# Second score half and second exponential moved ahead of the first sums and the first logarithm in a 64-step recurrent attention

## The chip, the core and the metric

The kernel runs on one core of one Trainium2 chip. The core has five engines with an instruction queue each: PE (TensorE, matmuls), ACT (ScalarE), DVE (VectorE), POOL (GpSimd) and SP (SyncE, which only issues transfers here). They are tied together by semaphores alone. The metric is the time of one execution on the device in microseconds (us), as the median of several runs; lower is better.

## The reference

The reference has two parts. A is an attention with a recurrent memory: the sequence of 2048 rows is cut into 64 segments of 32 rows, and each segment attends to itself and to 8 memory rows. The first 8 rows of a segment's output are the memory of the next, so the 64 steps can only run one after the other. B, a gated MLP with spatial mixing, comes after A and is not touched by the change.

```python
# A, cut: S 2048, Dm 512, H 32 heads, Dh 128, M 8 memory rows, seg_len 32
for s in range(n_seg):
    xs = x[:, s * seg_len:(s + 1) * seg_len, :].copy()
    h = jnp.concatenate([mem, xs], axis=1)
    q = jnp.einsum('btd,dhe->bhte', h, Wq)
    k = jnp.einsum('btd,dhe->bhte', h, Wk)
    v = jnp.einsum('btd,dhe->bhte', h, Wv)
    scores = jnp.einsum('bhqe,bhke->bhqk', q, k) * scale
    scores = jnp.where(mask[None, None], scores, -1000000000.0)
    p = _softmax(scores, axis=-1)
    o = jnp.einsum('bhqk,bhke->bhqe', p, v)
    o = jnp.einsum('bhte,hed->btd', o, Wo)
    mem = o[:, :M, :].copy()
    outs.append(o[:, M:, :])
```

## The kernel before

One segment is one pass of the loop over `s`. The 32 heads are dealt with in two halves of 16 (`b` 0 and 1). PE forms Q and K in five pieces; ACT copies each piece out of PSUM and DVE transposes it (`QK_evac`). Then come the scores of a half (`S_half`), their exponential on ACT (`sm_exp`), the sums of the exponentials on PE by a matmul with ones (`sm_sums`), and the reciprocal of the sums on ACT in two instructions, a logarithm (`sm_ln`) and an exponential of its negative (`sm_rcp`). `sm_norm` scales: DVE does the 160 columns of the segment's own keys, POOL the 64 columns of the memory keys. V is formed on PE beside this (`V_half`, `V_evac`), and `PV_half` multiplies. Both halves of `PV_half` are followed by copies to `cT`, by `Wo`, and by the new memory rows, which the next segment's Q and K need.

Each small matmul uses 32 of the array's 128 columns. Groups of four (`c` 0 to 3) lie on the four column strips. `held=True` keeps the weights that the strip has already, so nothing is loaded.

A small emitter orders the work. Each engine runs its instructions in the order in which they are written. The emitter works out what each has to wait for; a PSUM bank is one unit in this, whatever columns are used. A PE instruction that would need more than one wait hands all but one on to an earlier PE instruction that has none:

```python
    def finalize(self):
        ...
        pe = self.by_eng["pe"]
        for op in pe:
            while len(op.waits) > 1:
                d = op.waits[-1]
                t = next((p for p in reversed(pe[max(0, op.pos - 60):op.pos]) if not p.waits and p.gidx > d.gidx), None)
                if t is None:
                    break
                op.waits.pop()
                t.waits = [d]
        ...
```

The parts of the segment that the change touches (all that `SB`, `UBK`, `VB`, `PVB` name are PSUM banks):

```python
    QKP = ((0, 0, 8, 0, 0), (0, 0, 8, 1, 1), (1, 0, 8, 0, 6), (1, 0, 4, 1, 7), (1, 4, 4, 1, 2))
    SB = 5
    UBK = (0, 1)
    PVB = (0, 1, 6, 7)
    VB = {(0, 0): 6, (1, 0): 7, (1, 2): 2}
    ...
    def QK(s, k, dc, first=0, last=3, held=False):
        b, p0, np_, mi, bank = QKP[k]
        sl = slot(s)
        ws = (w_q, w_k)[mi]
        h0, nh = 16 * b + 2 * p0, 2 * np_
        for c in range(4):
            rhs = ws[:, dc, :].rearrange("p (h c i) -> p c h i", c=4, i=32)[:, c, h0:h0 + nh, :]
            pe(lambda e, c=c, rhs=rhs: mm(e, held, ps[32 * c:32 * c + 32, bank, 0:32 * nh], hT[:, sl, dc, :], rhs,
                                          dc == first, dc == last, (0, 32 * c)),
               reads=[("hTx", (s // 4) % 3), ("hTm", s, dc // 2), ("W", mi, 2 * b), ("W", mi, 2 * b + 1)], writes=[PB(bank)])

    def QK_evac(piece):
        b, p0, np_, mi, bank = piece
        st_ = Tst[:, mi, 64 * p0:64 * (p0 + np_)]
        tok = [("T", mi, k) for k in halves(b, p0, np_)]
        act(lambda e: e.activation(out=st_.rearrange("p (hp i r) -> p hp i r", i=32, r=2),
                                   in_=ps[:, bank, 0:64 * np_].rearrange("p (hp r i) -> p hp i r", r=2, i=32), func=ACT.Copy),
            reads=[PB(bank)], writes=tok)
        src = st_.bitcast(U32)
        dt_, nm = ((QT, "QT"), (KT, "KT"))[mi]
        dst = dt_[:, b, p0:p0 + np_, :, :].rearrange("p hp q r -> p (hp q r)").bitcast(U32)
        if mi == 0:
            dst = dst.rearrange("p (hp q) -> p hp q", hp=np_)[:, :, 8:40]
        dve(lambda e: e.transpose(out=dst, in_=src), reads=tok, writes=[(nm, b, k) for k in halves(b, p0, np_)])
    ...
    def S_half(s, b):
        ...
        rd = [(n, b, k) for n in ("QT", "KT") for k in range(2)] + [("QTe", b)]
        for g in range(4):
            for c in range(4):
                hp, r = 2 * c + g // 2, g % 2
                pe(lambda e, hp=hp, r=r, c=c, g=g: e.matmul(
                    ps[32 * c:32 * c + 32, SB, c0 + g * 40:c0 + (g + 1) * 40], lhsT=KT[:, b, hp, :, r], rhs=QT[:, b, hp, :, r],
                    start=False, stop=(g == 3), skip_group_check=True, tile_position=(0, 32 * c)),
                    reads=rd, writes=[PB(SB)])
        ...   # four more matmuls (L601), 64 columns each, against the memory keys
    def sm_exp(b):
        act(lambda e: e.activation(out=E_sb[:, b, :], in_=ps[:, SB, 224 * b:224 * b + 224], func=ACT.Exp, scale=scale, bias=SHIFT),
            reads=[PB(SB)], writes=[("E", b), ("Ex", b)])

    def sm_sums(b):
        bank = UBK[b]
        for c in range(4):
            q = slice(32 * c, 32 * c + 32)
            pe(lambda e, q=q, c=c: e.matmul(ps[q, bank, 224:384], lhsT=ones[:, q], rhs=E_sb[:, b, 0:160], start=True, stop=False,
                                            skip_group_check=True, tile_position=(0, 32 * c)),
               reads=[("E", b), "ones"], writes=[PB(bank)])
        for c in range(4):
            q = slice(32 * c, 32 * c + 32)
            pe(lambda e, q=q, c=c: mm(e, True, ps[q, bank, 224:384].rearrange("p (g q) -> p g q", q=40)[:, :, 0:16], ones[:, q],
                                      E_sb[:, b, 160:224].rearrange("p (g q) -> p g q", q=16), False, True, (0, 32 * c)),
               reads=[("Ex", b), "ones"], writes=[PB(bank)])

    def sm_ln(b):
        bank = UBK[b]
        act(lambda e: e.activation(out=R_sb[:, b, :], in_=ps[:, bank, 224:384], func=ACT.Ln, scale=LNS),
            reads=[PB(bank)], writes=[("R", b)])

    def sm_rcp(b):
        act(lambda e: e.activation(out=R_sb[:, b, :], in_=R_sb[:, b, :], func=ACT.Exp, scale=-1.0, bias=RBIAS),
            reads=[("R", b)], writes=[("R", b)])

    def sm_norm(b):
        dve(lambda e: e.tensor_tensor(out=E_sb[:, b, 0:160], in0=R_sb[:, b, :], in1=E_sb[:, b, 0:160], op=ALU.mult),
            reads=[("R", b), ("E", b)], writes=[("E", b)])
        ev = E_sb[:, b, 160:224].rearrange("p (g q) -> p g q", q=16)
        rv = R_sb[:, b, :].rearrange("p (g q) -> p g q", q=40)[:, :, 0:16]
        pool(lambda e: e.tensor_tensor(out=ev, in0=rv, in1=ev, op=ALU.mult),
             reads=[("R", b), ("Ex", b)], writes=[("Ex", b)])

    def V_half(s, b, gs, dc, first=0, last=3, held=False):
        bank = VB[b, gs[0]]
        sl = slot(s)
        w = 128 * (gs[1] - gs[0])
        for c in range(4):
            c0 = (16 * b + 4 * c + gs[0]) * DH
            pe(lambda e, c=c, c0=c0: mm(e, held, ps[32 * c:32 * c + 32, bank, 0:w], hT[:, sl, dc, :], w_v[:, dc, c0:c0 + w],
                                        dc == first, dc == last, (0, 32 * c)),
               reads=[("hTx", (s // 4) % 3), ("hTm", s, dc // 2), ("W", 2, 2 * b), ("W", 2, 2 * b + 1)], writes=[PB(bank)])

    def V_evac(b, eng, gs=(0, 4)):
        bank = VB[b, gs[0]]
        dst, src = V_sb[:, b, 128 * gs[0]:128 * gs[1]], ps[:, bank, 0:128 * (gs[1] - gs[0])]
        tok = [("V", b, g) for g in range(*gs)]
        if eng == "act":
            act(lambda e: e.activation(out=dst, in_=src, func=ACT.Copy, scale=VSC), reads=[PB(bank)], writes=tok)
        else:
            dve(lambda e: e.tensor_scalar(out=dst, in0=src, scalar1=VSC, scalar2=None, op0=ALU.mult), reads=[PB(bank)], writes=tok)

    def PV_half(s, b):
        xb = s % NVX
        for g in range(4):
            for c in range(4):
                q = slice(32 * c, 32 * c + 32)
                c0 = 160 * b + 40 * g
                pe(lambda e, q=q, c=c, g=g, c0=c0: e.matmul(
                    ps[:, PVB[c], c0:c0 + 40], lhsT=V_sb[q, b, g * 128:(g + 1) * 128], rhs=E_sb[q, b, g * 40:(g + 1) * 40],
                    start=(g == 0), stop=False, skip_group_check=True, tile_position=(32 * c, 0)),
                    reads=[("V", b, g), ("E", b)], writes=[PB(PVB[c])])
        for c in range(4):
            q = slice(32 * c, 32 * c + 32)
            pe(lambda e, q=q, c=c: e.matmul(
                ps[:, PVB[c], 160 * b:160 * b + 160].rearrange("p (g q) -> p g q", q=40)[:, :, 0:16], lhsT=Vx[q, xb, b, :],
                rhs=E_sb[q, b, 160:224].rearrange("p (g q) -> p g q", q=16),
                start=False, stop=True, skip_group_check=True, tile_position=(32 * c, 0)),
                reads=[("Vx", xb, b), ("Ex", b)], writes=[PB(PVB[c])])
```

The middle of the loop body:

```python
        QK_evac(QKP[2])
        QK(s, 3, 0, held=True)
        QK(s, 4, 0, last=2, held=True)
        QK(s, 3, 1)
        QK(s, 4, 1, last=2, held=True)
        QK(s, 3, 2)
        QK(s, 3, 3)
        QK_evac(QKP[3])
        QK(s, 4, 3, last=2, held=True)
        QK(s, 4, 2, last=2)
        lastop["k"] = em.by_eng["pe"][-1]
        QK_evac(QKP[4])
        if s == NSEG - 1:
            load_wT(0, [lastop["q"]])
        if s == 0:
            mask_pe()
        S_half(s, 0)
        sm_exp(0)
        for dc in range(DC):
            V_half(s, 0, (0, 4), dc)
        V_evac(0, "dve")
        sm_sums(0)
        sm_ln(0)
        S_half(s, 1)
        lastop["s"] = em.by_eng["pe"][-1]
        sm_exp(1)
        sm_rcp(0)
        if s == NSEG - 1:
            sp(lambda e: e.dma_start(w_in1, winr[:, :, 0:FH]), writes=["w_in1"], after=[lastop["s"], lastop["x"]])
            sp(lambda e: e.dma_start(bsp_b, bass.AP(B_b_sp.tensor, B_b_sp.offset, [[0, 128], [1, S]])), writes=["bsp"], after=[lastop["k"]])
            for r in range(8, RB - 2):
                xn2T_dma(r, [lastop["s"], lastop["x"]])
        V_half(s, 1, (0, 2), 3, 3, 0)
        V_half(s, 1, (2, 4), 3, 3, 0, held=True)
        V_half(s, 1, (0, 2), 2, 3, 0)
        V_half(s, 1, (2, 4), 2, 3, 0, held=True)
        V_half(s, 1, (0, 2), 1, 3, 0)
        V_half(s, 1, (0, 2), 0, 3, 0)
        sm_norm(0)
        sm_sums(1)
        sm_ln(1)
        sm_rcp(1)
        V_half(s, 1, (2, 4), 0, 3, 1)
        V_half(s, 1, (2, 4), 1, 3, 1)
        lastop["v"] = em.by_eng["pe"][-1]
        V_evac(1, "dve", (0, 2))
        V_evac(1, "act", (2, 4))
        sm_norm(1)
        ...   # up to two groups of four filler matmuls, two of another kind
        PV_half(s, 0)
        PV_half(s, 1)
        ...   # two more filler groups
        cT_evac(0, "act", (0,))
        ...   # seven more copies, then Wo, the new memory and the next segment
```

Filler matmuls are work for later segments or earlier rows (L498, L751, L289 with hTe), put where PE would otherwise wait. Even segments have four 512-column fillers more than odd ones.

Of the kernel before, what the change touches and what calls it, by code (L numbers as in the profile page):

```python
# [178 lines left out]
def fast_path(nc, st, keep, A_x, A_mem0, A_Wq, A_Wk, A_Wv, A_Wo, A_seg_len, B_w_in, B_w_sp, B_b_sp, B_w_out, out):  # L179
# [25 lines left out]
    em = Emitter(n_dma_sems=40)  # L205
# [72 lines left out]
    def PB(b):  # L278
        return ("ps", b)
# [4 lines left out]
    def pe(fn, **k):  # L284
        return em.add("pe", fn, **k)

    def mm(e, hold, out, lhsT, rhs, start, stop, pos):
        if not hold:
            return e.matmul(out, lhsT=lhsT, rhs=rhs, start=start, stop=stop, skip_group_check=True, tile_position=pos)  # L289
        return e.add_instruction(mybir.InstMatmult(  # L290
            name=nc.get_next_instruction_name(), engine=mybir.EngineType.PE, ins=[e.lower_ap(rhs), e.lower_ap(lhsT)], outs=[e.lower_ap(out)],
            start_tensor_calc=start, stop_tensor_calc=stop, tile_size=(128, 32), tile_position=pos, bass_skip_group_check=True,
            ldweights=False))

    def act(fn, **k):
        return em.add("act", fn, **k)

    def dve(fn, **k):
        return em.add("dve", fn, **k)

    def pool(fn, **k):
        return em.add("pool", fn, **k)
# [109 lines left out]
    def slot(s):  # L412
        return s % NSLOT
# [127 lines left out]
# [10 lines that stand above are left out]
# [4 lines left out]
# [13 lines that stand above are left out]
# [39 lines left out]
# [52 lines that stand above are left out]
# [273 lines left out]
    lastop = {}  # L932
    wq = []
    qx_copy(0)
    for s in range(NSEG):
# [31 lines left out]
        lastop["q"] = em.by_eng["pe"][-1]  # L967
        QK_evac(QKP[2])
        QK(s, 3, 0, held=True)
        QK(s, 4, 0, last=2, held=True)  # L970
        QK(s, 3, 1)
        QK(s, 4, 1, last=2, held=True)
        QK(s, 3, 2)
        QK(s, 3, 3)
        QK_evac(QKP[3])
        QK(s, 4, 3, last=2, held=True)
        QK(s, 4, 2, last=2)
        lastop["k"] = em.by_eng["pe"][-1]
        QK_evac(QKP[4])
        if s == NSEG - 1:  # L980
# [5 lines left out]
        for dc in range(DC):  # L986
            V_half(s, 0, (0, 4), dc)
        V_evac(0, "dve")
        sm_sums(0)
        sm_ln(0)  # L990
        S_half(s, 1)
        lastop["s"] = em.by_eng["pe"][-1]
        sm_exp(1)
        sm_rcp(0)
        if s == NSEG - 1:
            sp(lambda e: e.dma_start(w_in1, winr[:, :, 0:FH]), writes=["w_in1"], after=[lastop["s"], lastop["x"]])
            sp(lambda e: e.dma_start(bsp_b, bass.AP(B_b_sp.tensor, B_b_sp.offset, [[0, 128], [1, S]])), writes=["bsp"], after=[lastop["k"]])
# [4 lines left out]
        V_half(s, 1, (0, 2), 2, 3, 0)  # L1002
        V_half(s, 1, (2, 4), 2, 3, 0, held=True)
        V_half(s, 1, (0, 2), 1, 3, 0)
        V_half(s, 1, (0, 2), 0, 3, 0)
        sm_norm(0)
        sm_sums(1)
        sm_ln(1)
        sm_rcp(1)
        V_half(s, 1, (2, 4), 0, 3, 1)  # L1010
        V_half(s, 1, (2, 4), 1, 3, 1)
        lastop["v"] = em.by_eng["pe"][-1]
        V_evac(1, "dve", (0, 2))
        V_evac(1, "act", (2, 4))
        sm_norm(1)
        if s + 1 < NSEG:
# [949 lines left out]
def build_kernel(nc, A_x, A_mem0, A_Wq, A_Wk, A_Wv, A_Wo, A_seg_len, B_x, B_w_in, B_w_sp, B_b_sp, B_w_out, out):  # L1966
    args = (A_x, A_mem0, A_Wq, A_Wk, A_Wv, A_Wo, A_seg_len, B_w_in, B_w_sp, B_b_sp, B_w_out, out)
    with contextlib.ExitStack() as keep:
        with contextlib.ExitStack() as st:
            em, sems, dsems, flag = fast_path(nc, st, keep, *args)  # L1970
# [88 lines left out]
```

The softmax here doesn't subtract the row's maximum and nothing guards it: scores larger than these inputs give would overflow.

## Time and profile before

| What | Value |
|---|---|
| median of 3 runs | 851.51 us (851.4 to 854.64) |
| profiled execution, first to last instruction | 848.4 us |
| granted TensorE clock in it | 0.999 |
| first score matmul of segment 0 | 49.1 us |
| first score matmul of segment 63 | 667.3 us |
| from one segment's to the next, most segments | 9.72 to 9.78 us |

The table is read so: the setup takes the first 49 us, the 64 segments some 628 us, and part B the rest. The page's first block gives each engine's busy time with its share of the span and its number of instructions. PE's time is that of matmuls, PEld's that of weight loads, which run beside them; matmuls are pipelined and their ends are modelled, so their starts are the better guide. A timeline line has the start in us, the time taken, the engine, the line of the kernel, the operation, what it writes and reads with partitions x elements, the count of instructions drawn together, and in brackets the engine's idle time before it with the one that ended it. Line numbers are those of the kernel before: L289 and L290 are the matmuls of Q, K and V (L290 those with held weights, and the second part of the sums), L559 and L567 the copy and the transpose in `QK_evac`, L595 and L601 the scores, L608 the exponential, L615 the sums, L626 the logarithm, L630 the reciprocal, L634 and L638 the scaling on DVE and POOL, L656 and L658 the V copies, L666 and L672 the products of `PV_half`, L574 the copy of the next segment's memory queries on POOL. A line of a stretch has, for each engine, its busy time and the number of its instructions.

### The profile page before, as it was taken

The numbers are of one execution on the slowest core, as the hardware profiler recorded it, in microseconds if no ns is written. First come the engines' busy times: TensorE is split into PE (matmuls) and PEld (weight loads), VectorE is DVE, ScalarE is ACT, GpSimd is POOL, SyncE is SP. The second block draws the span as 40 slices with busy tenths as digits, with TensorE's granted clock in tenths as the row PEclk, the third lists the DMA queues.
The fourth block names the chain that finished last, engine by engine and source line by source line (L and its number), as shares of the span: only waits on it lengthen the run. The fifth ranks groups of instructions, "written<-read, shape, count | busy, mean of one in ns | idle before, by whom it ended". The sixth has DMA issues, their size and how long they took to land.

```text
span 848.4 us, 46072 instructions
## 1 busy us (share of the span) xinstructions
PE 834.1 (98%) x22552; PEld 438.3 (52%) x19480; DVE 515.3 (61%) x1322; ACT 471.7 (56%) x1367; POOL 168.7 (20%) x425
## 2 busy tenths in 40 slices
PE   8889999999999999999999999999999999999998
PEld 8545555555545555555555555555555544444443
DVE  3456666676666666666766666666666664453443
ACT  3446666766667676667666666767666755300000
POOL 7312212121212122221222121122111232100000
PEclk9999999999999999999999999999999999999999
DMA  9972220222332221322222324242321690033001
GB/s 319 392 231 75 69 74 28 60 72 61 77 92 58 50 66 43 75 38 61 60 73 73 95 57 80 60 94 72 58 52 56 188 280 7 1 112 106 32 12 40
DMA packets 112920, 75.25 MB, mean 89 GB/s; under 512 B 70728, under 2 KB 98512, under 8 KB 112720
## 3 DMA queue, kind: packets, MB, share of 16 engines
q1 hardware_dynamic: 111504, 70.88, 30.2%
q8 instruction: 166, 2.72, 1.3%
q0 software_dynamic: 384, 1.05, 0.3%
q10 hardware_dynamic: 832, 0.33, 0.1%
q14 instruction: 34, 0.28, 0.1%
HBM read 39.46 MB, written 20.58 MB: 71 GB/s over the span
## 4 chain that ended last, share of the span: by engine, by line
PE 92%; SPq 5%; DMA 1%; issue 0%; DVE 0%; ACT 0%
PE f_ps L289 33%; PE f_ps L701 14%; PE f_ps L290 12%; PE f_ps L1172 11%; PE f_ps L751 3%; PE f_ps L666 3%; PE f_ps L1165 3%; PE f_ps L1248 3%; SPq L329 3%; PE f_ps L1129 3%; PE f_ps L498 2%; DMA f_arena<-in_A_Wo_dram 1%; SPq L825 1%; PE f_ps L595 1%; PE f_ps L615 1%; PE f_ps L672 1%
## 5 line engine op out<-in xcount | busy, mean ns | idle before, releaser
L289 PE MATMUL f_ps<-f_arena,f_hT 128*32 128x512 bf16 (+1 forms) x5632 | 359.7, 331 | 0.3
L289 PEld LDWEIGHTS f_ps<-f_arena,f_hT 128*32 128x32 bf16 x5632 | 133.1, 96 | 161.6 <-issue 69.8
L290 PE MATMUL f_ps<-f_arena,f_hT 128*32 128x512 bf16 (+1 forms) x2560 | 188.5, 315 | 0.0
L559 ACT ACTIVATE f_Tst<-f_ps 128x512 bf16<-128x512 f32 (+1 forms) x320 | 149.7, 510 | 57.6 <-PE f_ps L289 53.9
L701 PE MATMUL f_ps<-f_arena,f_cT 128*32 128x256 bf16 x4096 | 130.6, 274 | 0.9 <-DMA f_arena<-in_A_Wo_dram 0.6
L638 POOL TENSOR_TENSOR f_E_sb<-f_R_sb,f_E_sb 128x64 bf16<-128x64 f32 x128 | 57.0, 446 | 362.1 <-ACT f_R_sb L630 362.1
L567 DVE STREAM_TRANSPOSE f_QT<-f_Tst 128x256 uint32<-128x256 uint32 x128 | 57.1, 446 | 94.3 <-ACT f_Tst L559 94.3
L701 PEld LDWEIGHTS f_ps<-f_arena,f_cT 128*32 128x32 bf16 x4096 | 90.0, 94 | 37.1 <-ACT f_cT L686 23.2
L1172 PE MATMUL f_ps<-f_arena 128*128 128x512 bf16 x448 | 100.6, 379 | 0.0
L688 DVE TENSOR_SCALAR f_cT<-f_ps 128x160 bf16<-128x160 f32 x256 | 65.2, 318 | 35.2 <-PE f_ps L672 35.2
L713 ACT ACTIVATE f_part<-f_ps 128x256 bf16<-128x256 f32 x128 | 49.1, 383 | 57.7 <-PE f_ps L701 53.7
L658 DVE TENSOR_SCALAR f_V_sb<-f_ps 128x512 bf16<-128x512 f32 (+1 forms) x128 | 71.1, 555 | 13.6 <-PE f_ps L289 13.6
L686 ACT ACTIVATE f_cT<-f_ps 128x160 bf16<-128x160 f32 x256 | 57.1, 310 | 36.3 <-PE f_ps L672 36.3
L1172 PEld LDWEIGHTS f_ps<-f_arena 128*128 128x128 bf16 x448 | 43.8, 98 | 52.8
L567 DVE STREAM_TRANSPOSE f_KT<-f_Tst 128x128 uint32<-128x128 uint32 (+1 forms) x192 | 65.9, 356 | 2.8
L626 ACT ACTIVATE f_R_sb<-f_ps 128x160 f32<-128x160 f32 x128 | 38.9, 304 | 34.8 <-PE f_ps L290 34.8
L634 DVE TENSOR_TENSOR f_E_sb<-f_R_sb,f_E_sb 128x160 bf16<-128x160 f32 x128 | 41.7, 326 | 23.4 <-ACT f_R_sb L630 23.4
L1178 DVE TENSOR_TENSOR f_arena<-f_ps,f_arena 128x512 f32<-128x512 f32 x28 | 19.3, 690 | 54.4 <-PE f_ps L1172 52.4
L289 PE MATMUL f_ps<-f_arena,f_hTe 128*32 128x512 bf16 x640 | 48.8, 382 | 0.0
L608 ACT ACTIVATE f_E_sb<-f_ps 128x224 bf16<-128x224 f32 x128 | 45.9, 359 | 0.1
L751 PE MATMUL f_ps<-f_arena,f_cTx 128*32 128x512 bf16 x512 | 43.9, 379 | 0.5 <-issue 0.4
L630 ACT ACTIVATE f_R_sb<-f_R_sb 128x160 f32<-128x160 f32 x128 | 42.6, 332 | 2.0
(123 smaller groups left out, 1027.3 us busy)
## 6 DMA issues: line engine op xcount, KB each, us to landing
wT_d<-f_wst SPq DMA_DIRECT2D x32, 256.0 KB
f_arena<-wT_d SPq DMA_DIRECT2D x32, 256.0 KB
f_arena<-in_A_Wv_dram SPq DMA_DIRECT2D x4, 1024.0 KB
f_arena<-in_A_Wk_dram SPq DMA_DIRECT2D x4, 1024.0 KB
f_arena<-in_A_Wo_dram SPq DMA_DIRECT2D x4, 1024.0 KB
f_Vx<-vext_d SPq DMA_DIRECT2D x124, 32.0 KB
f_arena<-in_A_Wq_dram SPq DMA_DIRECT2D x3, 1024.0 KB
vext_d<-f_Vs SPq DMA_DIRECT2D x20, 128.0 KB
```

The source lines that it names most:

```text
L289: return e.matmul(out, lhsT=lhsT, rhs=rhs, start=start, stop=stop, skip_group_check=True, tile_position=pos)
L290: return e.add_instruction(mybir.InstMatmult(name=nc.get_next_instruction_name(), engine=mybir.EngineType.PE, ins=[e.lower_ap(rhs), e.lowe ...
L559: act(lambda e: e.activation(out=st_.rearrange("p (hp i r) -> p hp i r", i=32, r=2), in_=ps[:, bank, 0:64 * np_].rearrange("p (hp r i) -> ...
L567: dve(lambda e: e.transpose(out=dst, in_=src), reads=tok, writes=[(nm, b, k) for k in halves(b, p0, np_)])
L638: pool(lambda e: e.tensor_tensor(out=ev, in0=rv, in1=ev, op=ALU.mult), reads=[("R", b), ("Ex", b)], writes=[("Ex", b)])
L658: dve(lambda e: e.tensor_scalar(out=dst, in0=src, scalar1=VSC, scalar2=None, op0=ALU.mult), reads=[PB(bank)], writes=tok)
L686: act(lambda e: e.activation(out=dst, in_=src, func=ACT.Copy, scale=UNSC), reads=[PB(PVB[c])], writes=tok)
L688: dve(lambda e: e.tensor_scalar(out=dst, in0=src, scalar1=UNSC, scalar2=None, op0=ALU.mult), reads=[PB(PVB[c])], writes=tok)
L701: pe(lambda e, h=h, g=g, i=i, b=b, c=c: e.matmul(ps[32 * g:32 * g + 32, bank, 0:d1 - d0], lhsT=cTh[:, i, 8:40], rhs=w_o[:, h, d0:d1], star ...
L713: act(lambda e: e.activation(out=part[:, s % 8, d0:d1], in_=ps[:, bank, 0:d1 - d0], func=ACT.Copy), reads=[PB(bank)], writes=[("part", s % ...
L751: pe(lambda e, h=h, g=g, i=8 * qr + bg: e.matmul(ps[32 * g:32 * g + 32, WXB, :], lhsT=cTx[:, rb % 2, i, :], rhs=w_o[:, h, :], start=(i < 4 ...
L1172: pe(lambda e: e.matmul(ps[:, bank, 0:TB], lhsT=z2[:, sc, fb * 128:(fb + 1) * 128], rhs=wTb[tb % 2][:, :, sc, :], start=(sc == 0), stop=(s ...
```

## The change

Only the order of instructions in the loop body changes; no instruction is added or taken away, and all operands stay the same.

- The last K piece (`QK(s, 4, ...)`) had two of its four groups behind the last of K piece 3; now it has three there, and ends alone. That lets the copy of piece 3 start earlier.
- `S_half(s, 1)` comes directly behind the V matmuls of the first half, ahead of the first sums. On ACT `sm_exp(1)` thus comes ahead of `sm_ln(0)`. It is meant to have the second exponential ready earlier, so that the second sums need no wait.
- The second sums and their logarithm are written one V group earlier, and both reciprocals (`sm_rcp`) come after both logarithms.
- The groups of the second V half are in another order, so that one more keeps its weights where K keeps one less; its first copy on DVE is written ahead of the scaling.

```diff
--- before.py
+++ after.py
@@ -967,14 +967,14 @@
         lastop["q"] = em.by_eng["pe"][-1]
         QK_evac(QKP[2])
         QK(s, 3, 0, held=True)
-        QK(s, 4, 0, last=2, held=True)
+        QK(s, 4, 0, last=1, held=True)
         QK(s, 3, 1)
-        QK(s, 4, 1, last=2, held=True)
         QK(s, 3, 2)
         QK(s, 3, 3)
         QK_evac(QKP[3])
-        QK(s, 4, 3, last=2, held=True)
-        QK(s, 4, 2, last=2)
+        QK(s, 4, 3, last=1, held=True)
+        QK(s, 4, 2, last=1)
+        QK(s, 4, 1, last=1)
         lastop["k"] = em.by_eng["pe"][-1]
         QK_evac(QKP[4])
         if s == NSEG - 1:
@@ -986,12 +986,11 @@
         for dc in range(DC):
             V_half(s, 0, (0, 4), dc)
         V_evac(0, "dve")
-        sm_sums(0)
-        sm_ln(0)
         S_half(s, 1)
         lastop["s"] = em.by_eng["pe"][-1]
+        sm_sums(0)
         sm_exp(1)
-        sm_rcp(0)
+        sm_ln(0)
         if s == NSEG - 1:
             sp(lambda e: e.dma_start(w_in1, winr[:, :, 0:FH]), writes=["w_in1"], after=[lastop["s"], lastop["x"]])
             sp(lambda e: e.dma_start(bsp_b, bass.AP(B_b_sp.tensor, B_b_sp.offset, [[0, 128], [1, S]])), writes=["bsp"], after=[lastop["k"]])
@@ -1002,15 +1001,16 @@
         V_half(s, 1, (0, 2), 2, 3, 0)
         V_half(s, 1, (2, 4), 2, 3, 0, held=True)
         V_half(s, 1, (0, 2), 1, 3, 0)
-        V_half(s, 1, (0, 2), 0, 3, 0)
-        sm_norm(0)
         sm_sums(1)
         sm_ln(1)
+        V_half(s, 1, (2, 4), 1, 3, 0)
+        V_half(s, 1, (0, 2), 0, 3, 0)
+        V_evac(1, "dve", (0, 2))
+        V_half(s, 1, (2, 4), 0, 3, 0, held=True)
+        lastop["v"] = em.by_eng["pe"][-1]
+        sm_rcp(0)
+        sm_norm(0)
         sm_rcp(1)
-        V_half(s, 1, (2, 4), 0, 3, 1)
-        V_half(s, 1, (2, 4), 1, 3, 1)
-        lastop["v"] = em.by_eng["pe"][-1]
-        V_evac(1, "dve", (0, 2))
         V_evac(1, "act", (2, 4))
         sm_norm(1)
         if s + 1 < NSEG:
```

## The prediction

> **What bounds the kernel now.** I read the page first, then the busy time of two neighbouring steps, the timeline of one step engine by engine, and last the list of waits. The recurrence is a loop of 64 steps. A step is counted here from its first score matmul (L595) to the next step's; the one that starts at 412.30 us has 9.72 us, its even neighbour 9.74.
>
> ```profile
> PE 834.1 (98%) x22552; PEld 438.3 (52%) x19480; DVE 515.3 (61%) x1322; ACT 471.7 (56%) x1367; POOL 168.7 (20%) x425
> ```
> ```profile
> 402.56:412.30 9.74, 9.74 (x340) 5.08 (x285) 6.84 (x20) 6.12 (x19) 2.48 (x6) 1.00 0.20 51
> 412.30:422.02 9.72, 9.70 (x336) 5.08 (x281) 7.02 (x20) 6.12 (x19) 2.48 (x6) 1.00 0.26 78
> ```
>
> PE at 98% looks like the bound, but the second view says otherwise: the even step has four matmuls of 512 columns more (x340 against x336), worth 0.22 us at the pace of L498 (eight in 0.43 us), and is only 0.02 us longer. So the odd step waits on a chain, and the even one has the chain and PE nearly level. The timeline shows which chain:
>
> ```profile
> 412.30 0.27 PE L595 MATMUL f_ps<-f_QT,f_KT 128*32 128x40 bf16 x16
> 412.44 1.03 PE L289 MATMUL f_ps<-f_arena,f_hT 128*32 128x512 bf16 x16
> 413.30 0.24 PE L615 MATMUL f_ps<-f_E_sb,f_ones 128*32 128x160 bf16 x4
> 413.39 0.27 PE L595 MATMUL f_ps<-f_QT,f_KT 128*32 128x40 bf16 x16
> 414.21 0.25 PE L615 MATMUL f_ps<-f_E_sb,f_ones 128*32 128x160 bf16 x4
> 415.62 0.27 PE L666 MATMUL f_ps<-f_E_sb,f_V_sb 32*128 32x40 bf16 x16
> 415.79 0.21 PE L672 MATMUL f_ps<-f_E_sb,f_Vx 32*128 32x64 bf16 x4
> ```
> ```profile
> 412.85 0.37 ACT L608 ACTIVATE f_E_sb<-f_ps 128x224 bf16<-128x224 f32 x1
> 413.61 0.30 ACT L626 ACTIVATE f_R_sb<-f_ps 128x160 f32<-128x160 f32 x1 [0.39 <-PE f_ps L290]
> 413.81 0.35 ACT L608 ACTIVATE f_E_sb<-f_ps 128x224 bf16<-128x224 f32 x1
> 414.05 0.33 ACT L630 ACTIVATE f_R_sb<-f_R_sb 128x160 f32<-128x160 f32 x1
> 414.53 0.30 ACT L626 ACTIVATE f_R_sb<-f_ps 128x160 f32<-128x160 f32 x1 [0.15 <-PE f_ps L290]
> 414.87 0.34 ACT L630 ACTIVATE f_R_sb<-f_R_sb 128x160 f32<-128x160 f32 x1
> ```
> ```profile
> 414.46 0.45 POOL L638 TENSOR_TENSOR f_E_sb<-f_R_sb,f_E_sb 128x64 bf16<-128x64 f32 x1 [3.47 <-ACT f_R_sb L630]
> 415.28 0.45 POOL L638 TENSOR_TENSOR f_E_sb<-f_R_sb,f_E_sb 128x64 bf16<-128x64 f32 x1 [0.38 <-ACT f_R_sb L630]
> 415.79 0.40 POOL L574 COPY f_QT<-f_arena 128x256 bf16<-128x256 bf16 x1
> ```
> ```profile
> 412.73 0.59 DVE L567 STREAM_TRANSPOSE f_KT<-f_Tst 128x128 uint32<-128x128 uint32 x2
> ```
>
> From here on, times count from 412.30. The second sums (L615) start at 1.91, the second logarithm (L626) at 2.23, its reciprocal (L630, an exponential) at 2.57; that ends at 2.91, POOL scales the memory part of the second half from 2.98 to 3.43, and the last product of that half (L672) starts at 3.49, 0.06 after POOL. Then come cT, Wo, the new memory and the next step, all behind it. The two POOL instructions lie 0.38 us apart with POOL idle between, each 0.08 after its own reciprocal.
>
> **What the Trainium skill says.** Its page "TensorE: Matmul & The Clock Gate", section "The mechanism", says that matmuls on different column strips overlap, about 4 ns apart, but start and end strictly in program order. The trace agrees: 16 matmuls of 512 columns, four per strip, take 0.86 us from their start to the next group's (412.44 to 413.30), so a strip is held 0.215 us by one. "GPSIMD Engine Reference", section 3.1, says that POOL is about half as fast as VectorE on a two-input elementwise operation and pays more per instruction; here POOL takes 0.45 us for 64 elements per partition and DVE (L634) 0.33 for 160. "Advanced Engine Details and Errata", section "Sequencer Loop", has instructions queued for their engine, where they wait for their semaphore; the trace shows ACT waiting 0.39 and 0.15 for the sums with other work behind. I take it that nothing overtakes.
>
> **The change, part by part.** The number of matmuls is the same, and so is the number that keep their weights: one held group less in K, one more in V. So no work goes; there are only moves.
>
> 1. *Last K piece alone at the end.* K piece 3 is complete one group of 256 columns (0.11 us) sooner. In the trace its copy (L559) starts 0.33 after its last group of matmuls does (group at -0.32, copy at 0.01). Now that group is at -0.43, so ACT starts the copy at -0.10; piece 4, last group at -0.11 in both kernels, is copied from 0.22 to 0.60, where ACT used to be busy with piece 3 (0.29 to 0.67). The first exponential comes at 0.49, before at 0.55. DVE's second KT transpose ends at 0.95 instead of 1.02 (0.31 each, 0.03 after ACT).
>
> 2. *Second score half ahead of the first sums.* By order it would start when the V matmuls leave PE, at 1.00. It needs that transpose: 0.95 + 0.06 = 1.01. That alone would be almost no wait. But its first matmul now waits for two engines, DVE (KT) and ACT (it writes the bank that the first exponential reads). The emitter leaves one wait on a matmul and moves the other to the nearest earlier matmul without one: here the sixteenth of the V group, on strip 3. In the built instruction order this stands in all 64 steps, and in none of the kernel before. That V matmul would start at 0.79; now it starts at 1.01 and holds strip 3 until 1.01 + 0.215 = 1.22. The score matmuls go round the four strips in order, so the fourth stops there until 1.22, and all behind it. From there to the next group it was 0.12 (1.09 to 1.23, less the first three), so the first sums start at 1.34.
>
> 3. *Sums, exponentials, logarithms.* First sums 0.10, five V groups 5 x 0.11: the second sums would be at 1.34 + 0.10 + 0.545 = 1.98. The second exponential starts 0.21 after the last score matmul's start (1.32, so 1.55), ends at 1.90, and lets the second sums go at 1.95; PE is later, so 1.98, against 1.91 before. The earlier exponential is thus eaten by the late score half. The second logarithm follows 0.32 after its sums, at 2.30.
>
> 4. *Reciprocals behind both logarithms.* ACT takes them in program order, so the first, which began at 1.75, now waits behind the second logarithm: 2.30 + 0.20 (the interval from a logarithm to the next independent instruction, 413.61 to 413.81) = 2.50, ending at 2.83. The second needs 0.23 more (start 2.73, end 3.06).
>
> 5. *POOL.* The two POOL instructions used to be apart; now both follow the first reciprocal: 2.83 + 0.08 = 2.91, + 0.446 = 3.36, + 0.065 from one POOL instruction to the next (before L574 it is 0.06), + 0.446 = 3.86. The last L672 starts at 3.86 + 0.06 = 3.92. DVE's two scalings, behind the V copy, end near 3.43, so the rest of PV is there in time; POOL ends last.
>
> Before, that L672 was at 3.49 in odd and 3.48 in even steps. The step grows by 0.43 to 0.44 us. Filler matmuls cannot absorb it: Wo waits for the cT copies, which wait for this L672. In 64 steps: 64 x 0.435 = 27.8 us, so 851.5 + 27.8 = 879.3; I say 879.
>
> **Rivals.** (a) *As meant*: nothing but the exponential moves and the second sums start at 1.78 instead of 1.91. If the chain followed by 0.13, odd steps would gain that and even ones 0.02 (PE), 32 x 0.15 = 4.8 us, about 847. Against it stand two orders that are in the code, not guessed: reciprocals behind logarithms, and POOL one after the other. (b) *POOL alone*: the displaced wait costs nothing, for instance because KT is ready by 0.79. Then the second sums are at 1.78, and every later time is 0.20 lower: L672 at 3.72, 0.235 a step, 866.5. Against it: DVE cannot have the transposes done by 0.79, as piece 4 is copied only after the last K matmul. (c) *Displaced wait alone*: POOL's record is longer than its work, and only the second reciprocal counts. It ends at 3.06, L672 is at 3.64, 0.15 a step, 861. Against it: POOL's recorded end and the L672 behind it lie 0.06 apart in odd and even steps alike, although PE arrives differently. (d) *Worse*: DVE's transposes run without overlap and KT comes at 1.03; then 0.08 more a step, 884.
>
> **Range and chances.** Each delay above is good to about 0.02 us, and there are five in a row, say 0.06 a step or 4 us; the displaced wait may also be milder. So 869 to 886. The border of 2% is 868.5, or 0.266 us a step: over it lie the main line and (d), under it (b) and (c). Chances: faster by over 2% 0.01, within 2% 0.12, slower 0.87.
>
> **What would show it.** Right: a step of about 10.16 us, odd and even alike; the two L638 back to back, with an idle time before the second under 0.1 us instead of 0.38; L630 twice in a row behind two L626; a gap of about 0.2 us inside the V group ahead of the second L595; L672 0.06 after POOL. PE's share falls, its busy work being the same. Wrong: second sums at 1.8 from the step's start (then step 2 fails), or PV's last product well after POOL's end (another engine is last), or a step under 9.9 us.

## The result

| | before | after |
|---|---|---|
| median, run beside each other | 853.03 us | 875.25 us |
| ratio, 95% interval | | 1.0259 (1.0231 to 1.0286) |
| profiled execution | 848.4 us | 873.6 us |
| a step, odd / even (median of steps 8 to 59) | 9.724 / 9.763 us | 10.161 / 10.160 us |

The change made the kernel 2.6% slower. Run again beside later experiments, the two gave 1.0237 (1.0213 to 1.0260). The first block of the page after counts the same instructions as the one before, but for 22545 matmuls on record instead of 22552, though the change takes none away. PE still shows 98%:

```profile
PE 859.0 (98%) x22545; PEld 458.9 (53%) x19480; DVE 511.7 (59%) x1322; ACT 464.9 (53%) x1367; POOL 159.8 (18%) x425
```

The busy times of two neighbouring steps, an odd one first, then an even one:

```profile
406.91:417.07 10.16, 10.15 (x336) 5.41 (x282) 6.30 (x18) 6.50 (x21) 1.55 (x4) 1.00 0.10 26
417.07:427.23 10.16, 10.16 (x340) 5.45 (x286) 6.78 (x20) 6.02 (x20) 2.33 (x6) 1.00 0.19 45
```

The even step has its four fillers more as before, and no time more at all: both now hang on the chain. PE counts as busy throughout although its work is the same: the modelled ends lie 0.2 to 0.4 us behind the starts, so gaps shorter than that do not show. The busy share tells little here, the starts tell the rest. Times below count from the step's first score matmul, here 406.92. PE, in the odd step:

```profile
407.05 1.26 PE L289 MATMUL f_ps<-f_arena,f_hT 128*32 128x512 bf16 x16
407.93 0.41 PE L595 MATMUL f_ps<-f_QT,f_KT 128*32 128x40 bf16 x13
408.15 0.21 PE L601 MATMUL f_ps<-f_QT,f_arena 128*32 128x64 bf16 x3
408.18 0.18 PE L595 MATMUL f_ps<-f_QT,f_KT 128*32 128x40 bf16 x1
408.19 0.24 PE L615 MATMUL f_ps<-f_E_sb,f_ones 128*32 128x160 bf16 x3
...
408.95 0.25 PE L615 MATMUL f_ps<-f_E_sb,f_ones 128*32 128x160 bf16 x4
...
410.83 0.21 PE L672 MATMUL f_ps<-f_E_sb,f_Vx 32*128 32x64 bf16 x4
```

The V group lasts 1.26 us instead of 1.03: one of its sixteen is late. The score matmuls, once one run of 16, now come in pieces, 13 and then the stragglers of one strip. The second sums stand at 2.04 (before 1.91), the last L672 at 3.92 (before 3.48). The list of waits has a line that the kernel before has not, a V weight load that waits for the K transpose, once in each step:

```profile
PEld f_ps L289 <- DVE f_KT L567: 21.8, 64, 0.4
```

ACT, then POOL, then DVE's K transposes, in the same step:

```profile
408.54 0.36 ACT L608 ACTIVATE f_E_sb<-f_ps 128x224 bf16<-128x224 f32 x1 [0.77 <-PE f_ps L290]
408.80 0.30 ACT L626 ACTIVATE f_R_sb<-f_ps 128x160 f32<-128x160 f32 x1
409.27 0.30 ACT L626 ACTIVATE f_R_sb<-f_ps 128x160 f32<-128x160 f32 x1 [0.18 <-PE f_ps L290]
409.47 0.55 ACT L630 ACTIVATE f_R_sb<-f_R_sb 128x160 f32<-128x160 f32 x2
```
```profile
409.88 0.90 POOL L638 TENSOR_TENSOR f_E_sb<-f_R_sb,f_E_sb 128x64 bf16<-128x64 f32 x2 [7.42 <-ACT f_R_sb L630]
```
```profile
407.27 0.60 DVE L567 STREAM_TRANSPOSE f_KT<-f_Tst 128x128 uint32<-128x128 uint32 x2
```

The second exponential, meant to come earlier, starts at 1.63 (before 1.51), with ACT idle for 0.77 us before it. The reciprocals stand side by side, and the two POOL instructions follow each other with no idle time that the view would name.

### The profile page after: what moved, and what is told of

It reads as the page before. It is cut to its first block, busy times and chain, and to the rows that moved or that the text cites. A ratio compares the mean times of both kernels' runs of the same rounds, so it can differ in the third digit from the quotient of the medians.

```text
span 873.6 us, 46065 instructions
## 1 busy us (share of the span) xinstructions
PE 859.0 (98%) x22545; PEld 458.9 (53%) x19480; DVE 511.7 (59%) x1322; ACT 464.9 (53%) x1367; POOL 159.8 (18%) x425
## 3 DMA queue, kind: packets, MB, share of 16 engines
q0 software_dynamic: 384, 1.05, 0.3%
## 4 chain that ended last, share of the span: by engine, by line
PE 93%; SPq 3%; DMA 2%; DVE 1%; issue 1%; ACTq 0%; ACT 0%
PE f_ps L289 32%; PE f_ps L701 13%; PE f_ps L290 11%; PE f_ps L1172 11%; PE f_ps L666 3%; PE f_ps L751 3%; PE f_ps L1165 3%; PE f_ps L1248 3%; PE f_ps L595 2%; PE f_ps L1129 2%; SPq L329 2%; PE f_ps L498 2%; PE f_ps L672 2%; DMA f_arena<-in_A_Wk_dram 2%; PE f_ps L615 1%; PE f_ps L601 1%
## 5 line engine op out<-in xcount | busy, mean ns | idle before, releaser
L289 PE MATMUL f_ps<-f_arena,f_hT 128*32 128x512 bf16 (+1 forms) x5632 | 371.8, 331 | 0.2
L289 PEld LDWEIGHTS f_ps<-f_arena,f_hT 128*32 128x32 bf16 x5632 | 152.4, 96 | 168.2 <-issue 69.4
L290 PE MATMUL f_ps<-f_arena,f_hT 128*32 128x512 bf16 (+1 forms) x2560 | 198.2, 315 | 0.0
L638 POOL TENSOR_TENSOR f_E_sb<-f_R_sb,f_E_sb 128x64 bf16<-128x64 f32 x128 | 48.1, 376 | 397.6 <-ACT f_R_sb L630 388.4
L595 PE MATMUL f_ps<-f_QT,f_KT 128*32 128x40 bf16 x2048 | 48.3, 182 | 0.3 <-DVE f_KT L567 0.3
L626 ACT ACTIVATE f_R_sb<-f_ps 128x160 f32<-128x160 f32 x128 | 38.5, 301 | 11.5 <-PE f_ps L290 11.5
```

Source lines behind the costliest of these rows:

```text
L290: return e.add_instruction(mybir.InstMatmult(name=nc.get_next_instruction_name(), engine=mybir.EngineType.PE, ins=[e.lower_ap(rhs), e.lowe ...
L595: pe(lambda e, hp=hp, r=r, c=c, g=g: e.matmul(ps[32 * c:32 * c + 32, SB, c0 + g * 40:c0 + (g + 1) * 40], lhsT=KT[:, b, hp, :, r], rhs=QT[: ...
```

## The experiments

The theory was that two things make up the loss, each worth about half: the wait that the emitter hands to a V matmul, and the first reciprocal behind the second logarithm, which puts the two POOL instructions one after the other at the end of the chain. The rivals were that only one of them counts, or that the new K and V grouping costs PE time. All values are medians over the odd steps 8 to 59, in us from the step's first score matmul; the ratio is to the kernel before, beside which each was timed. That one took 854.48 us beside e1 to e4, 855.24 beside e0 and e5 to e7, and 854.39 beside e8 and e9 (853.03 beside the change), so whole times expected from the first comparison come out 1.4 to 2.2 us low.

| Kernel | 2nd scores, strip 0 | 2nd sums | 2nd L638 | last L672 | step | ratio (95%) |
|---|---|---|---|---|---|---|
| before | 1.09 | 1.91 | 2.98 | 3.48 | 9.724 | 1 |
| after | 1.01 | 2.04 | 3.56 | 3.92 | 10.161 | 1.0259 (1.0231 to 1.0286) |
| e1_keep_wait | 1.10 | 1.90 | 3.41 | 3.78 | 10.019 | 1.0182 (1.0147 to 1.0217) |
| e2_rcp_back | 1.01 | 2.04 | 3.21 | 3.69 | 9.930 | 1.0135 (1.0102 to 1.0168) |
| e3_both | 1.10 | 1.89 | 3.07 | 3.55 | 9.790 | 1.0103 (1.0063 to 1.0144) |
| e4_before_rcp_late | 1.09 | 1.91 | 3.43 | 3.79 | 10.030 | 1.0165 (1.0129 to 1.0201) |
| e0_after_again | 1.01 | 2.04 | 3.55 | 3.92 | 10.158 | 1.0237 (1.0213 to 1.0260) |
| e5_carrier | 1.01 | 1.83 | 3.35 | 3.71 | 9.953 | 1.0116 (1.0091 to 1.0142) |
| e6_carrier_rcp | 1.01 | 1.83 | 3.01 | 3.48 | 9.726 | 1.0006 (0.9992 to 1.0020) |
| e7_no_pool0 | 1.01 | 2.04 | 3.19, alone | 3.70 | 9.945 | 1.0110 (1.0089 to 1.0130) |
| e8_k_alone | 1.09 | 1.91 | 2.98 | 3.48 | 9.727 | 1.0006 (0.9996 to 1.0017) |
| e9_s_ahead | 1.06 | 1.96 | 3.04 | 3.53 | 9.771 | 1.0035 (1.0018 to 1.0053) |

**e1_keep_wait.** The changed kernel; the first matmul of the second score half keeps both its waits.

```diff
-            while len(op.waits) > 1:
+            while len(op.waits) > 1 and op not in self.keep:
...
+        n0 = len(em.by_eng["pe"])
         S_half(s, 1)
+        em.keep.add(em.by_eng["pe"][n0])
```

> The changed kernel, with both waits left on the first matmul of the second score half instead of one handed on to the last V matmul. My theory (the handed-on wait holds column strip 3 for 0.2 us, and all later links of the chain move with it): the second sums move from 2.04 to about 1.80 us after the step's first score matmul, the last L672 from 3.92 to about 3.70, the step from 10.15 to about 9.93, so about 860 us. Rival A (only the late reciprocals and POOL count, the strip runs beside): no difference, 875. Rival B (two waits on one matmul cost PE as much as the handed-on one): 870 to 875, with the gap moved behind the V group.

It gained 0.14 us a step, not the 0.22 expected. The sixteenth V matmul started at 0.79 again and the sixteen score matmuls ran as one group, so part of the cost did lie in the held strip; but the scores came at 1.10, in the step at 423.10:

```profile
424.19 0.28 PE L595 MATMUL f_ps<-f_QT,f_KT 128*32 128x40 bf16 x16
```

KT was ready at the same time as in the changed kernel. So rival B holds in part: the two waits cost 0.09 us against one wait each (e5). The trace shows where the second wait went. PE's queue has an instruction of its own for it, once in each step, which neither the kernel before nor the changed one has:

```profile
L169 PEldq EVENT_SEMAPHORE  x64: 51/51/51, 50.0 to 685.8; - x64
```

The view gives its shortest, median and longest time in ns. It waits for DVE and lies at 0.99 to 1.04; the first weight load of the scores follows at 1.07, the first score matmul at 1.10. The instruction itself takes 0.05 of the 0.09; what makes up the rest is not shown.

**e2_rcp_back.** The changed kernel, the first reciprocal and its scaling ahead of the second logarithm again.

```diff
         sm_ln(0)
+        sm_rcp(0)
...
+        sm_norm(0)
         V_evac(1, "dve", (0, 2))
         V_half(s, 1, (2, 4), 0, 3, 0, held=True)
         lastop["v"] = em.by_eng["pe"][-1]
-        sm_rcp(0)
-        sm_norm(0)
         sm_rcp(1)
```

> The changed kernel, with the first reciprocal and its scaling put back ahead of the second logarithm; the handed-on wait stays. My theory (the two POOL instructions back to back end the chain): the first L638 comes early again, the second hangs on the second reciprocal alone; the second logarithm slips by 0.09 because ACT is then in the first reciprocal, L672 comes at about 3.69 instead of 3.92, the step takes about 9.93, so about 861 us. Rival (POOL's record is longer than its work, only the second reciprocal counts): the second reciprocal ends no earlier than now, so no gain, 875 or a little more.

The end of the second reciprocal, and the last products, in the step at 419.45:

```profile
422.21 0.34 ACT L630 ACTIVATE f_R_sb<-f_R_sb 128x160 f32<-128x160 f32 x1
```
```profile
423.13 0.21 PE L672 MATMUL f_ps<-f_E_sb,f_Vx 32*128 32x64 bf16 x4
```

L672 came at 3.69 and the odd step took 9.930, as expected to the digit. The second reciprocal still ended at 3.11, as in the changed kernel; only POOL's queue was shorter. That speaks against the rival. The whole time was 866.57 us, not 861, in part because the even steps took 9.991.

**e3_both.** e1 and e2 together.

> The changed kernel with both of these mended. My theory: the two costs add, second sums at 1.80, last L672 at about 3.47 (before: 3.49), a step of about 9.71; so 849 to 852 us, level with the kernel before: what the earlier exponential brings is taken back by the first reciprocal ahead of the second logarithm, and in even steps by PE's own work. Rival (something else in the change costs too, such as the K or V grouping): well above 853.

At 862.98 us it was 1% slower than before instead of level, and the rival's number came true. The score half at 1.10 (e1's finding) explains the odd steps: 9.790 against 9.726 in e6, which differs from this kernel only in that no matmul keeps two waits. That is 2 us in all. The other 6 or so are not explained by it: the even steps took 9.876, as long as in e6, and single steps of up to 10.9 us lie among the odd ones. As e6 has the same K and V grouping and comes out level, the rival's cause is not shown; the rest stays open.

**e4_before_rcp_late.** The kernel before, with the reciprocals late and nothing else of the change but the order of two DVE instructions.

```diff
-        sm_rcp(0)
...
-        sm_norm(0)
+        V_evac(1, "dve", (0, 2))
         sm_sums(1)
         sm_ln(1)
+        sm_rcp(0)
+        sm_norm(0)
         sm_rcp(1)
...
-        V_evac(1, "dve", (0, 2))
```

> The kernel before, with only the first reciprocal and its scaling put behind the second logarithm (and the first copy of the second V half ahead of that scaling on DVE, as in the changed kernel). My theory: the first reciprocal starts at 2.43 instead of 1.75, POOL's two instructions run back to back and end at about 3.73, L672 comes at 3.79 instead of 3.49: 0.30 a step, about 870 us. Rival (POOL is not the last link, the second reciprocal is): it ends about 0.1 later than before, so at most 0.09 a step, 857.

0.31 us a step, and L672 at 3.79: the late first reciprocal, with the POOL pair behind it, makes the kernel 1.65% slower by itself. In the step at 425.39, POOL, then PE:

```profile
428.23 0.90 POOL L638 TENSOR_TENSOR f_E_sb<-f_R_sb,f_E_sb 128x64 bf16<-128x64 f32 x2 [4.15 <-ACT f_R_sb L630]
```
```profile
429.18 0.21 PE L672 MATMUL f_ps<-f_E_sb,f_Vx 32*128 32x64 bf16 x4
```

POOL ends at 429.13, L672 starts 0.05 later. The second reciprocal ended at 2.99, 0.08 later than before; the rival would have that much for the whole loss.

**e0_after_again.** The changed kernel, beside e5 to e7.

> The changed kernel unaltered, run beside the next ones so that they can be compared on one chip. All theories: a step of 10.16 us, about 1.026 times the kernel before.

The step was the same to 0.003 us.

**e5_carrier.** The changed kernel, with a matmul of one column that carries the wait for ACT.

```diff
+        pe(lambda e: e.matmul(ps[0:32, SB, 448:449], lhsT=ones[:, 0:32], rhs=ones[:, 0:1], start=True, stop=True,
+                              skip_group_check=True, tile_position=(0, 0)), reads=["ones"], writes=[PB(SB)])
         S_half(s, 1)
```

> The changed kernel, with one matmul of a single column added between the V group and the second score half; it takes the wait for the first exponential, so that the score half keeps one wait and hands none to V. Leaving two waits on the score matmul had it start at 1.10 us instead of the 1.01 at which KT is ready. My theory (a handed-on wait holds strip 3, two waits on one matmul hold the queue, one wait on each is free): the second score half starts at 1.01 to 1.02, the second sums at about 1.80, the last L672 at about 3.69, the step at 9.93 or a little over where PE is level, so about 861 us and some 14 us under the changed kernel. Rival (the score half comes at 1.10 for another reason, such as the V group's own end): again 1.10, and 866.

PE in the step at 420.37, with the carrier at L989:

```profile
421.36 0.17 PE L989 MATMUL f_ps<-f_ones 128*32 128x1 bf16 x1
421.38 0.28 PE L595 MATMUL f_ps<-f_QT,f_KT 128*32 128x40 bf16 x16
...
421.52 0.24 PE L615 MATMUL f_ps<-f_E_sb,f_ones 128*32 128x160 bf16 x4
...
422.20 0.25 PE L615 MATMUL f_ps<-f_E_sb,f_ones 128*32 128x160 bf16 x4
```

The score half starts at 1.01 as one group, the first sums at 1.15, the second at 1.83. One wait less on a V matmul and one added matmul are worth 0.21 us a step. The scores start where expected, so the rival falls; sums, L672 and step come 0.02 to 0.03 later than expected. The ratio falls from 1.0237 to 1.0116 on the same chip.

**e6_carrier_rcp.** The carrier, and the first reciprocal back as in e2.

> The same carrier matmul, and the first reciprocal and its scaling put back ahead of the second logarithm. My theory: nothing is then left of the cost; last L672 at about 3.46 to 3.48 (before 3.48), odd steps at about 9.71, even ones held by PE at about 9.76; level with the kernel before, within 0.4%. Rival (the K and V grouping costs PE time): L672 as early, but the step over 9.80 in both kinds.

The last products, in the step at 414.69:

```profile
418.18 0.21 PE L672 MATMUL f_ps<-f_E_sb,f_Vx 32*128 32x64 bf16 x4
```

Level with the kernel before. L672 is at 3.48 again and the odd step at 9.726. So the two costs are, on balance, all there is in odd steps: 0.208 (the wait, after to e5) and 0.227 (reciprocal and POOL, e5 to e6) make 0.435 of the 0.437. The even steps took 9.88 rather than the 9.76 expected. Ten of the 26 took 9.77 to 9.80; most of the others have pauses of 0.1 to 0.2 us beyond the usual, ahead of the Wo matmuls or among them, at other places in other steps. Why is left open, and with it whether the K and V grouping costs PE something there. The times side by side do not show a loss: the interval of the ratio ends at 1.0020, which is 1.7 us, or 0.05 us for each even step (an estimate from these two numbers). The only trace of the kernel before is of an execution of 850.12 us, and its median beside e6 was 855.24, so it may well have had such pauses there too; no trace shows it.

**e7_no_pool0.** The changed kernel without POOL's scaling of the first half's memory columns, which thus enter the product unscaled: that part of the computation is left out.

> The changed kernel without POOL's scaling of the memory columns of the first half: those columns stay unscaled, so this part of the computation is left out. Everything else, the handed-on wait and the late reciprocals included, stays. My theory (the second POOL instruction waits for the first): the one that is left starts 0.08 after the second reciprocal's end, at 3.19 instead of 3.56, and takes 0.446; L672 at 3.69 instead of 3.92, the step at about 9.94 to 9.99, about 861 to 864 us. Rival (the second reciprocal or DVE's scaling sets the end): L672 no earlier than 3.85, 871 or more.

POOL in the step at 420.48, then PE:

```profile
423.67 0.46 POOL L638 TENSOR_TENSOR f_E_sb<-f_R_sb,f_E_sb 128x64 bf16<-128x64 f32 x1 [4.51 <-ACT f_R_sb L630]
```
```profile
424.18 0.21 PE L672 MATMUL f_ps<-f_E_sb,f_Vx 32*128 32x64 bf16 x4
```

The one left starts 0.08 after the second reciprocal's end, and L672 comes 0.22 sooner. Sums and reciprocals stand as in the changed kernel. DVE's second scaling ended 0.11 sooner, at 3.48, but in both kernels it ends before POOL does (3.59 against 3.86 there, 3.48 against 3.65 here), and L672 starts 0.06 after POOL's end. This shows that the wait is for the first POOL instruction.

**e8_k_alone.** The kernel before with the K groups of the change.

```diff
-        QK(s, 4, 0, last=2, held=True)
+        QK(s, 4, 0, last=1, held=True)
         QK(s, 3, 1)
-        QK(s, 4, 1, last=2, held=True)
...
-        QK(s, 4, 3, last=2, held=True)
-        QK(s, 4, 2, last=2)
+        QK(s, 4, 3, last=1, held=True)
+        QK(s, 4, 2, last=1)
+        QK(s, 4, 1, last=1)
```

> The kernel before, with only the K groups reordered so that the last K piece ends alone. My theory (it frees ACT's copies and the KT transpose by 0.06, which nothing in the old order waits for): the first exponential at 0.51 instead of 0.55, the second score half still at 1.09, the last L672 still at 3.48, the step as before; ratio 1.000, within 0.3%. Rival (the K grouping itself costs PE time): steps 0.05 or more longer, 0.4% or more slower.

Only the first exponential (0.55 to 0.51) and KT (1.01 to 0.95) moved; the later links stand where they were. The K grouping costs nothing that shows in the odd steps or the whole time and, alone, brings nothing.

**e9_s_ahead.** The kernel before with the second score half and exponential ahead, and the carrier.

```diff
-        sm_sums(0)
-        sm_ln(0)
+        pe(...)   # the carrier, as in e5
         S_half(s, 1)
         lastop["s"] = em.by_eng["pe"][-1]
+        sm_sums(0)
         sm_exp(1)
+        sm_ln(0)
         sm_rcp(0)
```

> The kernel before, with only the second score half ahead of the first sums and the second exponential ahead of the first logarithm, with the one-column carrier so that no wait is handed to V; K and V groups and the first reciprocal as before. My theory: KT is ready 0.06 later without the K grouping, so the score half comes at about 1.065; six V groups instead of five stand ahead of the second sums, which so come at about 1.96, later than the 1.91 before; L672 at about 3.53, a step some 0.05 longer, ratio 1.003 to 1.008. Rival (the earlier exponential shortens the step by itself): second sums at 1.83, step under 9.70 in odd steps, ratio under 0.998.

The second sums, in the step at 414.86:

```profile
416.83 0.24 PE L615 MATMUL f_ps<-f_E_sb,f_ones 128*32 128x160 bf16 x4
```

As expected: scores 1.06, second sums 1.96, 0.35% slower. The title's idea alone does not pay. The exponential comes 0.05 earlier, but PE is not ready for the sums; with the K and V grouping as well (e6) the sums gain 0.08, and the first reciprocal, now between the logarithms, costs ACT as much.

## Why the prediction held, step by step

1. *K piece.* Expected: first exponential at 0.49, KT ready at 0.95. Measured 0.51 and 0.95. Right, and worth nothing by itself (e8).

2. *The handed-on wait.* Expected: the sixteenth V matmul at 1.01, strip 3 blocked to 1.22, the scores stopped there, first sums at 1.34. Measured 1.01, then 1.23 for the first score matmul on strip 3. The size was right, a part of the picture was not: I had all strips stop with the fourth. Strips 0 to 2 ran on through their twelve score matmuls by 1.11. Then they did stop, until 1.24, just behind strip 3's first, and their first sums started at 1.28, ahead of two score matmuls of strip 3 that precede them in the program (the piecemeal lines of PE above). Strip 3's sums followed at 1.37. Without the handed-on wait, in e5, all four start at 1.15 to 1.16.

3. *Second sums.* Expected 1.98, with PE last. Measured 2.04, with the second exponential last: it started 0.29 after the last score matmul did, where I had taken 0.21 (and 1.32 + 0.21 is 1.53, not the 1.55 that I wrote), and ended at 1.98; the sums followed 0.05 later. The term was 0.08 short, the sums came 0.06 later than expected, and the limiting engine was ACT.

4. *Reciprocals.* Expected 2.50 and 2.73. Measured 2.56 and 2.79, the 0.06 of step 3 and no more.

5. *POOL.* Expected start 2.91, end of the second 3.86, L672 3.92. Measured 2.97, 3.86, 3.92. The agreement is partly luck: the second instruction ended 0.45 after the first, where I had 0.065 + 0.446 = 0.51. This cancels step 3's error. DVE's second scaling ended at 3.59, 0.16 later than expected, and still 0.27 before POOL.

6. *The sum.* Expected 0.435 a step in both kinds. Measured 0.437 in odd and 0.397 in even steps: the even ones began from 9.76, set by PE's own work and small pauses rather than by the chain. That makes 32 x 0.437 + 32 x 0.397 = 26.7 us instead of 27.8. In the profiles the 63 intervals from the first step's start to the last's grew by 24.5 us (618.2 to 642.7), where these medians make 26.3: single pauses, which fall in a few steps of every kernel, came to 1.8 us less in this one. The medians differ by 22.2: the profiled execution of the kernel before took 850.12 us, 2.9 under its median, that of the kernel after 875.34, as its median. So 879 was 4 us high, inside the range; from the 853.03 that ran beside the change, the expected growth of 27.8 was 5.6 too large. None of this touches the mechanism.

7. *The signs.* The long steps alike in odd and even, the pairs of L626 and L630, the gap inside the V group and the 0.06 from POOL to L672 came as expected. Two did not: PE's share stayed at 98%, because its modelled ends hide the gaps, and the record of the second L638 starts 0.14 after the end of the first, not under 0.1, and is the shorter for it (last section).

Of the rivals, (a) fell with e9 and e6: the earlier exponential, freed of both costs, only comes out level. (b) and (c) are each half of the truth, as e5, e7 and e4 show. The two halves added, since both lie on one chain. (d) did not come: KT was ready at 0.95.

## What to carry to other kernels

When an instruction is moved ahead, look at what it has to wait for in its new place: a wait that used to be covered by an earlier one becomes a second wait, and where a scheduler puts that may cost more than the move brings. When one of two parallel strands is postponed so that both end together, whatever they share behind (here POOL) becomes serial and goes onto the path. A small carrier instruction for the extra wait cost nothing that shows in the odd steps here (e6: 9.726 us, before 9.724).

## What the runs showed of the hardware

Column strips are less bound to program order than the prediction had it, but not free of each other. The Trainium skill, "TensorE: Matmul & The Clock Gate", section "The mechanism", has matmuls start and end strictly in program order. The lines of the kernel before that the prediction took as agreement show that the strips overlap, not that they keep this order. In the changed kernel nine score matmuls of strips 0 to 2 that stand behind strip 3's first one in the program started at 1.05 to 1.11 us, and that one at 1.23; and three sums started at 1.28, ahead of two score matmuls of strip 3 that come earlier in the program (1.29 and 1.31). Between 1.11 and 1.23, though, no score matmul started on any strip. The records name no strip; I tell them apart by number and order of the starts. What held strips 0 to 2 in that time is not shown.

A second wait left on a matmul became an instruction of its own in PE's queue, of 0.051 us, in all 64 steps of e1. The matmul started 0.09 us later than with the same waits on two matmuls (1.10 in e1, 1.01 in e5).

Two POOL instructions of 0.446 us, the second with its inputs ready, ended 0.449 us apart in the changed kernel, with the second recorded as 0.307 long from 0.143 after the first's end. In these traces a POOL record's length depends on what it follows; the distance of the ends is the safer figure.
